# Weight loads for the second expert, weight splits and number conversions at other steps, and a branch hint for two more engines

## The chip, the cores and the metric

The kernel runs on one core of a Trainium2 chip as one launch. The metric is the device time of a run in microseconds (us), the median over several runs. The core's engines have queues of their own, and the text calls them as the profile does: PE (matrix engine), PEld (its weight loads), DVE (vector), ACT (scalar), POOL (GpSimd) and SP (which here issues the weight loads). A trailing q, as in PEq, means the engine's sequencer: branches, semaphore waits and the like.

## The reference, cut to what matters

```
attn_out = _attn_ref(q, k, v, omega)          # 4 x 8 heads x 576 x 64, random features
x = attn_out ... reshape(2304, 512)
x = (x @ w_a * (x @ w_b)) @ w_out             # MoE 1: 512 -> 1536 -> 512, dense
logits = normalised x @ normalised expert_emb.T / tau
expert_idx = argmax(logits, axis=1)           # 8 experts
out[mask] = gate_w[mask] * (relu(x[mask] @ w1[e]) @ w2[e])   # MoE 2: w1 512x1024, w2 1024x512
```

All inputs are float32. Each product is made of three TensorE products, with every operand split into a rounded high part and the remainder.

## The kernel before

**Attention** (to about 198 us) and the conversion of the MoE 1 weights run first. The weights of w_a, w_b and w_out come in as 36 pieces (3 for each of 12 chunks `kf`) through a small staging ring `stg` and are rebuilt on the chip, one piece by one call of `conv()`: an ACT pass (line 235), two DVE passes `cv<-stg` (lines 236 and 238) and a POOL addition (line 240). When the 36th is done, `load_en` fetches the normalised expert embeddings back.

**MoE 1** runs over 6 units `u` of 384 tokens and, within each, the 12 chunks `kf`; step n is 12u + kf, and the first `ND` = 5 steps lie in the attention. In the loop of `run` each step n issues, in this order: the conversions that are due (the `while` of line 1153, whose formula decides how many each step gets), the split of the next chunk's weights (`chunk_ab`: ACT cast `abh`, line 562, and DVE subtraction `abl`, line 563), 24 matmuls `pA`, `pB` of this chunk (`ab_mm`, lines 595 to 597), the product `h` on DVE (line 611), its split `hh`, `hl`, and 9 matmuls `pO` (`out_mm`, line 627), of this or an earlier step. Each engine executes its instructions in the order in which the loop issues them. In units 1 to 5 DVE, ACT and POOL also compute the routing of the unit before (`route_plan`: scores in kf 1 to 8, softmax in kf 9, ranks and scatters behind).

In the last unit, kf 0 calls `alloc_stage` and loads both weights of the most used expert e0 into the staging tiles `st` (`load_w`: 4 DMAs of 512 KB for w1, line 901, and 8 of 256 KB for w2, line 905). At kf 8, 9, 10 and 11 a quarter of w1 each is split into `w1t` pairs (ACT cast and DVE subtraction of 128x1024).

**MoE 2** has a step 0 (320 tokens of e0), a step 1 (256 tokens of e0), and then bodies `body_b(j)`, of up to 16, one for each block of up to 320 tokens of one expert. In this input 7 run (`nB` = 7), and three experts occur. A step takes hidden blocks `p_h` (w1) and output blocks `p_o` (w2, tiles `w2t` and `w2u`), gathers rows by indirect DMAs on POOL (`rid`, then `xr<-yd,rid`), and scatters its result (`out_dram<-ob`). `after` is a piece of code that a step calls late: in step 0 it loads w1 of the second expert e1, in step 1 it is `first`, which loads w2 of that expert (and w1 only if the guess of e1 was wrong, `hn > 0`), and in the bodies it loads both weights of the expert after. The staging tiles are freed by the splits of the expert before. Bodies from `NSB_MIN` = 5 on stand in nested `If(nB > j)`, line 1313. Which width of a body runs is a branch on `kind` (lines 1298 and 1299). PE has a prefetch hint for the branch of line 1299 (`hint(j)`); no other engine has hints.

Of the kernel before, what the change touches and what calls it, by code (L numbers as in the profile page):

```python
# [17 lines left out]
ENG = mybir.EngineType  # L18
# [8 lines left out]
NU = NTILE // TU  # L27
KF = DFF // 128
# [4 lines left out]
NSB = 16  # L33
NSB_MIN = 5
NPRE = 24
# [4 lines left out]
ND = 5  # L40
# [60 lines left out]
class Kern:  # L101
# [790 lines left out]

    def alloc_stage(s):
        t = [s.x6("st", F32, (128, 1536)) for _ in range(6)]
        s.st1 = [t[k // 1][:, 0:1024] for k in range(4)]
        s.st2 = [t[k][:, 1024:1536] for k in range(4)] + [t[4][:, k:k + 512] for k in (0, 512, 1024)] + [t[5][:, 0:512]]
        s.x2 = t[5][:, 512:512 + XW]
# [12 lines left out]

    def alloc_w1(s):
        W = lambda: s.ab([128, 1024], F32R, "w1t")
        s.w1s = [(W(), W()) for _ in range(4)]

    def alloc_w2(s):
        W = lambda: s.ab([128, 2, 512], F32R, "w2t")
# [205 lines left out]
    def run(s):  # L1122
        nc, tc = s.nc, s.tc
        s.setup_consts()
        s.p0_consts()
        s.conv_open()
        x, ch, wo, hr, hs = {}, {}, {}, {}, {}

        def prep(n):
            if n in hr:  # L1130
                hs[n] = s.split_h(hr.pop(n))

        for t in s.attention():
            if TS - 2 <= t < TS:
                if t == TS - 2:
                    x[0], th = s.split_x(s.xraw[0])
                th.pop(0)()
            k, r = divmod(t - TS, TD)
            if 0 <= k < ND and r == 0:
                hr[k] = s.ab_mm(s.chunk_early(k), x[0])  # L1140
        xraw = s.xraw
        steps = [(u, kf) for u in range(NU) for kf in range(KF)]
        R = {}
        todo = {}
        en = s.setup_en()
        ch[ND] = s.chunk_ab(ND)
        done = 0
        for n, (u, kf) in enumerate(steps):
            if n < ND:
                continue  # L1150
            if n == ND:
                yield
            while s.n_conv < 3 * KF and s.n_conv < max(3 * (n + 2), NPRE + (3 * KF - NPRE) * (n + 1 - ND) // (KF - 2 - ND)):
                s.conv()
                if s.n_conv == 3 * KF:
                    s.load_en()
            next(en, None)
            if n + 1 < len(steps):
                ch[n + 1] = s.chunk_ab(steps[n + 1][1])
            if kf in (10, 11) and u + 1 < NU:  # L1160
                if kf == 10:
                    x[u + 1], xth = s.split_x(xraw[u + 1])
                xth.pop(0)()
            for f in todo.get(kf, []):
                f()
            if n == ND:
                wo[0] = s.chunk_wo(0)
                prep(0)
            hr[n] = s.ab_mm(ch.pop(n), x[u])
            if n - done <= 1:  # L1170
                prep(n)
            for f in todo.get(kf + 0.5, []):
                f()
            goal = n if u else (KF - 1) * (n + 1 - ND) // (KF - ND)
            while done < goal:
                s.out_mm(wo.pop(done), hs.pop(done), steps[done][1])
                done += 1
                wo[done] = s.chunk_wo(steps[done][1])
                prep(done)
            if kf == 0:  # L1180
                todo = s.route_plan(u - 1, R) if u else {}
            if u == NU - 1 and kf == 0:
                s.alloc_stage()
                s.load_w(s.e0v)
            if u == NU - 1 and kf == 8:
                s.alloc_w1()
            if u == NU - 1 and kf in (8, 9, 10, 11):
                s.split(*s.w1s[kf - 8], s.st1[kf - 8])
            if u == NU - 1 and kf == 6:
                s.alloc_x()  # L1190
                for i in range(SA):
                    s.ids_of(i, [s.idxa[:, t:t + 1] for t in range(3 * i, 5 if i else 3)])
            if u == NU - 1 and kf == 7:
                for i in range(SA):
                    for t in range(2 if i else 3):
                        s.gather(i, t, NT - 2 * TU * 128)
        n = len(steps) - 1
        s.alloc_p2()
        s.p_h = [s.psum("A", "p_h") for _ in range(3)]
        for t in range(3):  # L1200
            s.xT(0, t, s.p_h[t])
        s.out_mm(wo.pop(n), hs.pop(n), KF - 1)
        s.alloc_w2()
        s.split2(0, 4)
        s.alloc_h()
        s.queue_route(NU - 1, R)
        L = lambda ap, eng, hi: nc.values_load(ap, engines=eng, min_val=0, max_val=hi)  # L1207
        AD = [ENG.Activation, ENG.DVE]
        s.slot_now, s.early = 0, False
        ids_b = lambda j: s.ids_of(SA + j, [s.idxb[:, j, t:t + 1] for t in range(3)])  # L1210

        def idx_ready():
            if s.slot_now < 1:
                s.early = True
                return
            ids_b(0)
            for t in range(3):
                s.gather(SA, t)

        s.idx_ready = idx_ready  # L1220

        def next_xT(i, j):

            k = L(s.kind[0:1, j:j + 1], [ENG.PE] + AD, 2)

            def third(p, rest):
                with s.tc.If(k > 1) as c:
                    s.xT(i, 2, p[2])
                    rest()
                with c.Else():  # L1230
                    rest()
            return lambda p: xT2(i, p), third

        def xT2(i, p):
            for t in range(2):
                s.xT(i, t, p[t])

        s.step(0, 2, split2=lambda a, b: s.split2(a, b) if a else None, after=lambda: s.load_w1(s.e1v), nextx=lambda: (lambda p: xT2(1, p), None), bg=BG[0])
        s.slot_now = 1
        if s.early:  # L1240
            idx_ready()

        def hint(j):

            if j < NSB:
                k = L(s.kind[0:1, j:j + 1], [ENG.PE], 2)
                tc.mark_branch_hint_location(f"wide{j}", hint=k // 2, engines=[ENG.PE])

        def first():
            s.pump(1000)  # L1250
            s.alloc_b()
            ids_b(1)
            with tc.block():
                hint(0)
            hn = L(s.n0i[0:1, 1:2], [ENG.SP], 1)
            ne = L(s.n0i[0:1, 0:1], [ENG.SP], E - 1)
            with tc.If(hn > 0):
                s.load_w1(ne)
            s.load_w2(ne)

        def first1(f):
            f0 = L(s.fl[0:1, 0, 0:1], AD, 1)
            with tc.If(f0 > 0):
                s.split1(f)

        s.step(1, 1, after=first, split1=first1, nextx=lambda: next_xT(SA, 0), bg=BG[1])
        nB = L(s.nB[0:1, 0:1], mybir.ALL_ENGINES, NSB)

        def body_b(j):
            i = SA + j  # L1270
            new = L(s.fl[0:1, 0, j:j + 1], AD, 1)
            last = L(s.fl[0:1, 0, j + 1:j + 2], AD, 1)
            kind = L(s.kind[0:1, j:j + 1], mybir.ALL_ENGINES, 2)
            hn = L(s.fl[0:1, 1, j:j + 1], [ENG.SP], 1)
            ne = L(s.fl[0:1, 2, j:j + 1], [ENG.SP], E - 1)
            nx = None
            if j + 1 < NSB:
                for t in range(3):
                    s.gather(i + 1, t)
                x = next_xT(i + 1, j + 1)  # L1280
                nx = lambda: x
            if j + 2 < NSB:
                ids_b(j + 2)

            def sp2(a, b):
                with tc.If(new > 0):
                    s.split2(a, b)

            def sp1(f):
                with tc.If(last > 0):  # L1290
                    s.split1(f)

            def after():
                with tc.If(hn > 0):
                    s.load_w(ne)
                hint(j + 1)

            with tc.If(kind > 0) as c:
                with tc.If(kind > 1, label=f"wide{j}") as d:  # L1299
                    s.step(i, 2, sp2, sp1, after, nx)  # L1300
                with d.Else():
                    s.step(i, 1, sp2, sp1, after, nx)
            with c.Else():
                s.step(i, 0, sp2, sp1, after, nx)

        def rec_b(j):
            if j == NSB:
                return
            if j < NSB_MIN:
                body_b(j)  # L1310
                rec_b(j + 1)
            else:
                with tc.If(nB > j):  # L1313
                    body_b(j)
                    rec_b(j + 1)

        rec_b(0)
# [90 lines left out]
```

## Time and profile before

| | |
|---|---|
| median of 3 runs | 902.41 us (898.89, 902.41, 902.68) |
| the profiled execution's own time | 901.02 us |
| its span in the trace | 899.1 us |
| mean granted TensorE clock | 0.981 of full speed |
| busy: PE, DVE, ACT, POOL | 838.5, 595.2, 452.7, 348.6 us |

The span reaches from the first to the last traced instruction; the own time holds 1.9 us more. PE is busy 93% of the span, so time can go only where PE waits, where its clock is low, or after its last instruction.

### The profile page before, as it was taken

The page shows a single profiled execution, that of the slowest core. Times are in us where ns is not written, and L with a number is a line of the kernel's source. Part 1 is how long each engine was busy: PE and PEld are TensorE (multiplying, and loading weights), DVE is VectorE, ACT ScalarE, POOL GpSimd, SP SyncE. Part 2 cuts the span into 40 slices and gives each one's busy share as a digit, 9 for nine tenths or more (in the row PEclk, how much of TensorE's full clock was granted, in tenths as well). Part 3 has the DMA queues.
Part 4 walks back from the last instruction along what each step waited for, and adds up shares of the span by engine and source line. Part 5 has one row for each costly group of instructions (what it writes and reads, how often), then busy time and mean ns, then how long its engine had stood idle before and what let it go on. Part 6 is the DMA issues. An engine that isn't in the chain of part 4 may idle for free. (4 is left out here: it accounts for less than half of the span.)

```text
span 899.1 us, 15947 instructions
## 1 busy us (share of the span) xinstructions
PE 838.5 (93%) x5783; PEld 760.7 (85%) x5783; DVE 595.2 (66%) x1294; ACT 452.7 (50%) x1039; POOL 348.6 (39%) x332
## 2 busy tenths in 40 slices
PE   6989898899899999999999999999999799899991
PEld 5878787798799999999999999999888688799971
DVE  5899999857957865876786686687756434422220
ACT  4779888676445546545554654554622323311110
POOL 6576876503404313402512531255213433333330
PEclk9999999999999999999999999999999899999996
DMA  9564854302300010000001000502133721122220
GB/s 222 179 195 132 239 160 130 99 8 92 114 30 1 1 37 1 1 37 1 1 1 37 0 1 37 188 2 61 37 118 117 238 95 51 58 63 62 63 64 16
DMA packets 68355, 67.14 MB, mean 75 GB/s; under 512 B 27552, under 2 KB 56608, under 8 KB 68096
## 3 DMA queue, kind: packets, MB, share of 16 engines
q1 hardware_dynamic: 62784, 52.90, 19.4%
q0 software_dynamic: 5440, 12.68, 4.7%
q8 instruction: 60, 0.98, 0.5%
q14 instruction: 71, 0.58, 0.2%
HBM read 55.88 MB, written 9.68 MB: 73 GB/s over the span
## 5 line engine op out<-in xcount | busy, mean ns | idle before, releaser
L660 POOL TENSOR_TENSOR trp<-y,en 128x512 f32<-128x512 f32 x60 | 90.3, 1520 | 122.5 <-ACT trp L661 68.5
L1035 PE MATMUL p_h<-xth,w1t 128*128 128x256 f32 (+1 forms) x512 | 101.2, 293 | 7.9 <-DVE w2t L563 4.6
L562 ACT CAST hh<-h 128x384 fp32r<-128x384 f32 x72 | 37.1, 515 | 127.7 <-DVE h L611 127.7
L563 DVE TENSOR_TENSOR abl<-ab,abh 128x1024 fp32r<-128x1024 f32 x67 | 87.1, 1300 | 20.9 <-ACT abh L562 20.3
L597 PE MATMUL pB<-xuh,abl 128*128 128x384 f32 x288 | 96.9, 336 | 0.0
L390 ACT ACTIVATE p<-pj,nb 128x128 f32<-128x128 f32 x288 | 80.2, 396 | 26.2 <-DVE nb L379 16.1
L597 PE MATMUL pA<-xuh,abl 128*128 128x384 f32 x268 | 90.0, 336 | 1.4 <-DVE abl L563 1.4
L1035 PEld LDWEIGHTS p_h<-xth,w1t 128*128 128x128 f32 x512 | 83.1, 193 | 9.4 <-issue 9.1
L596 PE MATMUL pA<-xul,abh 128*128 128x384 f32 x268 | 90.1, 336 | 0.0
L595 PE MATMUL pA<-xuh,abh 128*128 128x384 f32 x268 | 90.1, 336 | 0.0
L595 PE MATMUL pB<-xuh,abh 128*128 128x384 f32 x268 | 89.5, 334 | 0.0
L596 PE MATMUL pB<-xul,abh 128*128 128x384 f32 x268 | 89.5, 334 | 0.0
L611 DVE TENSOR_TENSOR h<-pB,a 128x384 f32<-128x384 f32 x72 | 39.7, 552 | 63.3 <-PE pB L597 35.9
L1015 ACT ACTIVATE hT<-p_h 128x512 fp32r<-128x512 f32 (+1 forms) x42 | 22.5, 539 | 105.8 <-PE p_h L1035 70.9
L1035 PE MATMUL p_h<-xtl,w1t 128*128 128x256 f32 (+1 forms) x256 | 74.9, 293 | 0.0
L1020 DVE SCALAR_TENSOR_TENSOR hT<-p_h,hT 128x256 fp32r<-128x256 f32 (+2 forms) x52 | 25.0, 504 | 72.4 <-ACT hT L1015 42.5
L562 ACT CAST abh<-ab 128x1024 fp32r<-128x1024 f32 x67 | 70.3, 1049 | 0.5 <-PE pB L596 0.5
L653 DVE CUSTOM_DVE_ANT_0 trv<-y,en 128x512 bf16<-128x512 f32 x60 | 66.4, 1107 | 0.7
L627 PE MATMUL pO<-woh,hl 128*128 128x512 f32 x216 | 63.2, 401 | 2.8 <-DVE hl L563 2.8
L563 DVE TENSOR_TENSOR hl<-h,hh 128x384 fp32r<-128x384 f32 x72 | 40.5, 562 | 34.9 <-ACT hh L562 34.9
L627 PE MATMUL pO<-woh,hh 128*128 128x512 f32 x216 | 62.8, 399 | 0.4 <-ACT woh L562 0.4
L627 PE MATMUL pO<-wol,hh 128*128 128x512 f32 x216 | 62.5, 398 | 0.0
(237 smaller groups left out, 2133.9 us busy)
## 6 DMA issues: line engine op xcount, KB each, us to landing
stg<-in_moe_w_a_dram SPq DMA_DIRECT2D x12, 512.0 KB
stg<-in_moe_w_b_dram SPq DMA_DIRECT2D x12, 512.0 KB
stg<-in_moe_w_out_dram SPq DMA_DIRECT2D x12, 512.0 KB
st<-in_moe_w_dram SPq DMA_DIRECT2D x12, 512.0 KB
st<-in_moe_w_dram SPq DMA_DIRECT2D x24, 256.0 KB
yd<-y SPq DMA_DIRECT2D x6, 792.0 KB
v<-in_v_dram SPq DMA_DIRECT2D x16, 256.0 KB
q<-in_q_dram SPq DMA_DIRECT2D x8, 512.0 KB
```

The costliest lines, as they stand in the source:

```text
L390: s.nc.scalar.activation(out=s.p_[j][:, 4 * half + n], in_=pj[:, n * M:n * M + M], func=ACTF.Exp, bias=nb[:, n:n + 1])
L562: s.nc.scalar.copy(out=hi, in_=src)
L563: s.nc.vector.tensor_tensor(out=lo, in0=src, in1=hi.bitcast(F32), op=ALU.subtract)
L595: mm(out=out, lhsT=ah, rhs=wh, start=st, stop=False)
L596: mm(out=out, lhsT=ah, rhs=wl, start=False, stop=False)
L597: mm(out=out, lhsT=al, rhs=wh, start=False, stop=sp)
L611: nc.vector.tensor_tensor(out=h, in0=pp[1][:, :N], in1=a, op=ALU.mult)
L627: s.nc.tensor.matmul(out=s.po[j], lhsT=a[:, j * 128:j * 128 + 128], rhs=b, start=st, stop=sp)
L653: nc.vector.tensor_tensor_reduce(out=tr, in0=y[:, j, :DM], in1=s.en[:, e], scale=1.0, scalar=0.0, op0=ALU.mult, op1=ALU.add, accum_out=dt[ ...
L660: nc.gpsimd.tensor_tensor(out=tr, in0=y[:, j, :DM], in1=s.en[:, e], op=ALU.mult)
L1020: nc.vector.scalar_tensor_tensor(out=v, in0=pv[:, a - k0:b - k0], scalar=0.0, in1=h, op0=ALU.max, op1=ALU.subtract)
L1035: return lambda: nc.tensor.matmul(out=out, lhsT=a, rhs=b, start=st, stop=sp, skip_group_check=True)
```

## The change

It consists of four edits. In the MoE 1 loop the conversions are spread over one more step: the divisor in the formula becomes `KF - 1 - ND`. The four splits of w1 of e0 move from kf 8, 9, 10, 11 to kf 5, 7, 9, 11, and behind the last of them the loop now issues the four DMAs for w1 of e1. Step 0's `after` loads w2 of e1 in the place of w1, and `first` loads both only if the guess was wrong. Bodies from 4 on begin with a small block that gives POOL and DVE a prefetch hint on whether the next nested `If` is taken.

```
--- before.py
+++ after.py
@@ -892,6 +892,7 @@
 
     def alloc_stage(s):
         t = [s.x6("st", F32, (128, 1536)) for _ in range(6)]
+        s.w1s = []
         s.st1 = [t[k // 1][:, 0:1024] for k in range(4)]
         s.st2 = [t[k][:, 1024:1536] for k in range(4)] + [t[4][:, k:k + 512] for k in (0, 512, 1024)] + [t[5][:, 0:512]]
         s.x2 = t[5][:, 512:512 + XW]
@@ -910,7 +911,7 @@
 
     def alloc_w1(s):
         W = lambda: s.ab([128, 1024], F32R, "w1t")
-        s.w1s = [(W(), W()) for _ in range(4)]
+        s.w1s.append((W(), W()))
 
     def alloc_w2(s):
         W = lambda: s.ab([128, 2, 512], F32R, "w2t")
@@ -1150,7 +1151,7 @@
                 continue
             if n == ND:
                 yield
-            while s.n_conv < 3 * KF and s.n_conv < max(3 * (n + 2), NPRE + (3 * KF - NPRE) * (n + 1 - ND) // (KF - 2 - ND)):
+            while s.n_conv < 3 * KF and s.n_conv < max(3 * (n + 2), NPRE + (3 * KF - NPRE) * (n + 1 - ND) // (KF - 1 - ND)):
                 s.conv()
                 if s.n_conv == 3 * KF:
                     s.load_en()
@@ -1182,10 +1183,12 @@
             if u == NU - 1 and kf == 0:
                 s.alloc_stage()
                 s.load_w(s.e0v)
-            if u == NU - 1 and kf == 8:
+            if u == NU - 1 and kf in (5, 7, 9, 11):
+                k = (kf - 5) // 2
                 s.alloc_w1()
-            if u == NU - 1 and kf in (8, 9, 10, 11):
-                s.split(*s.w1s[kf - 8], s.st1[kf - 8])
+                s.split(*s.w1s[k], s.st1[k])
+                if k == 3:
+                    s.load_w1(s.e1v)
             if u == NU - 1 and kf == 6:
                 s.alloc_x()
                 for i in range(SA):
@@ -1235,7 +1238,7 @@
             for t in range(2):
                 s.xT(i, t, p[t])
 
-        s.step(0, 2, split2=lambda a, b: s.split2(a, b) if a else None, after=lambda: s.load_w1(s.e1v), nextx=lambda: (lambda p: xT2(1, p), None), bg=BG[0])
+        s.step(0, 2, split2=lambda a, b: s.split2(a, b) if a else None, after=lambda: s.load_w2(s.e1v), nextx=lambda: (lambda p: xT2(1, p), None), bg=BG[0])
         s.slot_now = 1
         if s.early:
             idx_ready()
@@ -1255,8 +1258,7 @@
             hn = L(s.n0i[0:1, 1:2], [ENG.SP], 1)
             ne = L(s.n0i[0:1, 0:1], [ENG.SP], E - 1)
             with tc.If(hn > 0):
-                s.load_w1(ne)
-            s.load_w2(ne)
+                s.load_w(ne)
 
         def first1(f):
             f0 = L(s.fl[0:1, 0, 0:1], AD, 1)
@@ -1268,6 +1270,9 @@
 
         def body_b(j):
             i = SA + j
+            if NSB_MIN <= j + 1 < NSB:
+                with tc.block():
+                    tc.mark_branch_hint_location(f"more{j + 1}", hint=nB > j + 1, engines=[ENG.Pool, ENG.DVE])
             new = L(s.fl[0:1, 0, j:j + 1], AD, 1)
             last = L(s.fl[0:1, 0, j + 1:j + 2], AD, 1)
             kind = L(s.kind[0:1, j:j + 1], mybir.ALL_ENGINES, 2)
@@ -1310,7 +1315,7 @@
                 body_b(j)
                 rec_b(j + 1)
             else:
-                with tc.If(nB > j):
+                with tc.If(nB > j, label=f"more{j}"):
                     body_b(j)
                     rec_b(j + 1)
```

The first place is DVE in unit 0 of MoE 1, near step 7. `cv<-stg` rows are conversions, `abl` the split of the next chunk, `h` the product.

```order
 L236 TENSOR_SCALAR cv<-stg 128x512
 L238 SCALAR_TENSOR_TENSOR cv<-stg,cv 128x512
-L236 TENSOR_SCALAR cv<-stg 128x512
-L238 SCALAR_TENSOR_TENSOR cv<-stg,cv 128x512
 L563 TENSOR_TENSOR abl<-ab,abh 128x1024
 L611 TENSOR_TENSOR h<-pB,a 128x384
```

One of three conversions left this step. One more leaves step 9 in the same way, and both come back in step 10:

```order
 L563 TENSOR_TENSOR hl<-h,hh 128x384
+L236 TENSOR_SCALAR cv<-stg 128x512
+L238 SCALAR_TENSOR_TENSOR cv<-stg,cv 128x512
+L236 TENSOR_SCALAR cv<-stg 128x512
+L238 SCALAR_TENSOR_TENSOR cv<-stg,cv 128x512
 L563 TENSOR_TENSOR abl<-ab,abh 128x1024
 L563 TENSOR_TENSOR xul<-xraw,xuh 128x768
```

Step 10 had no conversion before; now two stand ahead of its `abl`. The steps 5, 6 and 8 keep their two each.

The second place is SP, between the end of MoE 1 and step 0 of MoE 2. `yd<-y` are the last results of MoE 1 going to memory, a 128x1024 `st` is a quarter of w1, a 128x512 `st` an eighth of w2 (the changed file's line numbers are one higher here).

```order
 L701 DMA yd<-y 128x3x528
+L902 ISA
+L902 DMA st<-in_moe_w_dram 128x1024
+L902 ISA
+L902 DMA st<-in_moe_w_dram 128x1024
+L902 ISA
+L902 DMA st<-in_moe_w_dram 128x1024
+L902 ISA
+L902 DMA st<-in_moe_w_dram 128x1024
 L98 DMA yd<-y 128x3x528
```

The w1 load of e1 moved ahead of the last `yd<-y`; behind that row, where it stood, the eight DMAs of w2 stand now.

The third place is POOL at the start of body 4, behind the last scatter of body 3 in the program's text. It had this:

```order
L1117 DMA out_dram<-ob,xr 2304x512
L1298 ISA
L1298 UNCONDITIONAL_BRANCH
L1207 TENSOR_LOAD tb
L981 DMA xr<-yd,rid 128x528 x2
```

It now has this:

```order
L1118 DMA out_dram<-ob,xr 2304x512
L1303 ISA
L1303 UNCONDITIONAL_BRANCH
L1275 REGISTER_ALU
L1409 BRANCH_PREFETCH_HINT
L1274 UNCONDITIONAL_BRANCH
L1210 TENSOR_LOAD tb
L982 DMA xr<-yd,rid 128x528 x2
```

A comparison, the hint and a branch out of the block were added. DVE has the same three; PE, ACT and SP have only the added unconditional branch.

## Rows read from the trace of the kernel before

**Rows 1.** PE timeline, 223 to 237 us: start, duration, operation, idle before and releaser.
```profile
224.85 0.44 PE L597 MATMUL pA<-xuh,abl 128*128 128x384 f32 x1 [0.26 <-DVE abl L563]
...
234.51 1.65 PE L627 MATMUL pO<-woh,hl 128*128 128x512 f32 x3 [2.77 <-DVE hl L563]
```

**Rows 2.** DVE timeline, 217 to 225 us.
```profile
218.89 0.69 DVE L238 SCALAR_TENSOR_TENSOR cv<-stg,cv 128x512 int32<-128x512 int32 x1
...
221.55 0.41 DVE L236 TENSOR_SCALAR cv<-stg 128x512 int32<-128x512 int32 x1
222.00 1.67 DVE L238 SCALAR_TENSOR_TENSOR cv<-stg,cv 128x512 int32<-128x512 int32 x1
```

**Rows 3.** Windows: length, busy PE, PEld, DVE, ACT, POOL; PEclk; DMA; GB/s.
```profile
234.20:237.60 3.40, 3.09 (x8) 2.07 (x9) 1.60 (x4) 0.54 (x1) 0.00 (x0) 0.50 0.00 0
708.60:715.50 6.90, 5.22 (x24) 5.25 (x25) 2.32 (x4) 0.00 (x0) 2.04 (x2) 0.51 0.64 211
...
771.60:776.00 4.40, 4.38 (x37) 4.40 (x38) 2.73 (x5) 0.60 (x1) 3.48 (x4) 1.00 0.49 138
```

**Rows 4.** Timeline of all engines, 248 to 252 us.
```profile
248.66 0.56 DVE L611 TENSOR_TENSOR h<-pB,a 128x384 f32<-128x384 f32 x1 [0.70 <-PE pB L597]
...
249.73 0.55 DVE L563 TENSOR_TENSOR hl<-h,hh 128x384 fp32r<-128x384 f32 x1
...
251.20 0.86 PE L627 MATMUL pO<-woh,hl 128*128 128x512 f32 x3
```

**Rows 5.** PE timeline, 622 to 640 us, the rows with a wait.
```profile
626.86 0.44 PE L597 MATMUL pA<-xuh,abl 128*128 128x384 f32 x1 [0.50 <-DVE abl L563]
...
631.42 0.97 PE L627 MATMUL pO<-woh,hh 128*128 128x512 f32 x3 [0.39 <-ACT woh L562]
...
634.77 0.44 PE L597 MATMUL pA<-xuh,abl 128*128 128x384 f32 x1 [0.63 <-DVE abl L563]
```

**Rows 6.** DVE timeline, 604 to 638 us.
```profile
609.14 3.62 DVE L563 TENSOR_TENSOR abl<-ab,abh 128x1024 fp32r<-128x1024 f32 x1 [0.26 <-ACT abh L562]
...
625.59 1.22 DVE L563 TENSOR_TENSOR abl<-ab,abh 128x1024 fp32r<-128x1024 f32 x1
```

**Rows 7.** PE timeline, first matmul of body 0 and of body 2.
```profile
710.28 0.55 PE L1035 MATMUL p_h<-xth,w1t 128*128 128x256 f32 x1 [4.60 <-DVE w2t L563]
...
771.62 0.36 PE L1035 MATMUL p_h<-xth,w1t 128*128 128x256 f32 x1 [3.29 <-issue]
```

**Rows 8.** Line 1299 near 703, 764 and 839: count, duration ns min/median/max, first, last.
```profile
L1299 PEldq COMPARE_BRANCH  x1: 6890/6890/6890, 703.2 to 703.2; - x1
...
L1299 PEldq COMPARE_BRANCH  x2: 2127/3020/3914, 764.0 to 769.3; - x2
...
L1299 PEldq COMPARE_BRANCH  x1: 351/351/351, 839.6 to 839.6; - x1
```

**Rows 9.** SP timeline around steps 0 and 1: the loads for e1 (w2) and e2 (w1).
```profile
689.65 5.02 SPq L905 DMA_DIRECT2D st<-in_moe_w_dram  x8
...
699.10 2.68 SPq L901 DMA_DIRECT2D st<-in_moe_w_dram  x4
```

**Rows 10.** DMA view, 700 to 709 us: packets, MB, share of the 16 engines.
```profile
q1 hardware_dynamic: 572, 2.09, 66.5%
q0 software_dynamic: 270, 0.55, 16.4%
```

**Rows 11.** Windows as in Rows 3, at the end of step 1.
```profile
706.00:708.00 2.00, 0.00 (x0) 0.00 (x0) 0.47 (x1) 0.99 (x2) 0.00 (x0) 1.00 0.83 318
708.00:710.00 2.00, 0.00 (x0) 0.00 (x0) 1.58 (x3) 0.00 (x0) 0.00 (x0) 0.66 0.11 37
```

**Rows 12.** Lines 1313 and 1404 from 870 us on; columns as in Rows 8.
```profile
L1313 POOLq EVENT_SEMAPHORE  x5: 17/43/43, 887.2 to 887.6; - x5
...
L1313 POOLq COMPARE_BRANCH  x2: 43/46/50, 884.3 to 889.9; - x2
...
L1404 POOLq DRAIN  x3: 50/107/8239, 890.0 to 898.8; - x3
```

More of the change, by code (lines that the diff above doesn't have):

```diff
@@ L894, in alloc_stage @@
         t = [s.x6("st", F32, (128, 1536)) for _ in range(6)]
+        s.w1s = []
         s.st1 = [t[k // 1][:, 0:1024] for k in range(4)]
@@ L912, in alloc_w1 @@
         W = lambda: s.ab([128, 1024], F32R, "w1t")
-        s.w1s = [(W(), W()) for _ in range(4)]
+        s.w1s.append((W(), W()))
     def alloc_w2(s):
@@ L1152, in run @@
                 yield
-            while s.n_conv < 3 * KF and s.n_conv < max(3 * (n + 2), NPRE + (3 * KF - NPRE) * (n + 1 - ND) // (KF - 2 - ND)):
+            while s.n_conv < 3 * KF and s.n_conv < max(3 * (n + 2), NPRE + (3 * KF - NPRE) * (n + 1 - ND) // (KF - 1 - ND)):
                 s.conv()
@@ L1184, in run @@
                 s.load_w(s.e0v)
-            if u == NU - 1 and kf == 8:
+            if u == NU - 1 and kf in (5, 7, 9, 11):
+                k = (kf - 5) // 2
                 s.alloc_w1()
-            if u == NU - 1 and kf in (8, 9, 10, 11):
-                s.split(*s.w1s[kf - 8], s.st1[kf - 8])
+                s.split(*s.w1s[k], s.st1[k])
+                if k == 3:
+                    s.load_w1(s.e1v)
             if u == NU - 1 and kf == 6:
@@ L1236, in xT2 @@
                 s.xT(i, t, p[t])
-        s.step(0, 2, split2=lambda a, b: s.split2(a, b) if a else None, after=lambda: s.load_w1(s.e1v), nextx=lambda: (lambda p: xT2(1, p), None), bg=BG[0])
+        s.step(0, 2, split2=lambda a, b: s.split2(a, b) if a else None, after=lambda: s.load_w2(s.e1v), nextx=lambda: (lambda p: xT2(1, p), None), bg=BG[0])
         s.slot_now = 1
@@ L1257, in first @@
             with tc.If(hn > 0):
-                s.load_w1(ne)
-            s.load_w2(ne)
+                s.load_w(ne)
         def first1(f):
@@ L1270, in body_b @@
             i = SA + j
+            if NSB_MIN <= j + 1 < NSB:
+                with tc.block():
+                    tc.mark_branch_hint_location(f"more{j + 1}", hint=nB > j + 1, engines=[ENG.Pool, ENG.DVE])
             new = L(s.fl[0:1, 0, j:j + 1], AD, 1)
@@ L1312, in rec_b @@
             else:
-                with tc.If(nB > j):
+                with tc.If(nB > j, label=f"more{j}"):
                     body_b(j)
```

## The prediction

> **What bounds the kernel now.** The page's engine list comes first: PE is busy 93% of the span, no other engine over 66% but PE's own weight loads. So time can be had where PE waits, where its clock is low, or behind its last instruction. The chain of waits that ends last runs over the row gathers of the experts and does not show where PE loses time, so I read PE's timeline for rows with a wait ahead, then the windows for the clock, then the queue rows at the waits. The change touches four places.
>
> (A) In unit 0 of MoE 1 PE waits 0.26 us at 224.85 for `abl` and 2.77 at 234.51 for `hl`, both from DVE [rows 1]. Behind the second wait the granted clock is 0.50 for 3.40 us, the 1.2 GHz level, with 3.09 us of PE work in it [rows 3]; that work would have taken half as long at 2.4 GHz, so the fall costs 1.55.
>
> (B) In the last unit PE waits 0.50, 0.39 and 0.63 us [rows 5], 1.52 together.
>
> (C) Before body 0 PE waits 4.60 us, to 710.28 [rows 7]. The view puts this down to DVE's `w2t`, but the row that tells it is the branch of line 1299: PE's sequencer sat 6.89 us in it from 703.2, where the same line takes 2.1 to 3.9 at 764 to 769 and 0.35 at 839.6 [rows 8]. DMA was 0.83 busy in 706 to 708 and 0.11 in the two us behind [rows 11]; PE went on when the traffic was over. I take the branch to wait for its code, which comes by DMA, behind weights. The clock is then 0.51 for 6.90 us with 5.22 us of PE work [rows 3]: 2.6 lost. Together this place costs 7.2.
>
> (D) Behind PE's end POOL reaches its branch of line 1313 at 884.3 and its next semaphore instruction at 887.2, 2.9 us with nothing in between; it drains for 8.24 us from 890.0, and the span ends behind that [rows 12].
>
> **A: conversions.** Step 7 loses one of three conversions. Its DVE passes take 0.41 + 1.67 = 2.08 us (0.41 + 0.69 = 1.10 where the second pass is quick) [rows 2]. DVE runs through without a pause here, so everything behind comes 2.08 earlier, and so does the end of the wait at 234.51, which shrinks to 2.77 + 0.26 - 2.08 = 0.95. The waits of 0.39 to 0.63 [rows 5] are the nearest in size to it, and I take no fall of the clock behind it: 2.08 + 1.55 = 3.63. The price is step 10, which had no conversion and gets two, 2.2 to 4.2 us of DVE by the same passes, ahead of the `hl` that ended at 250.28 and was wanted at 251.20 [rows 4]: 0.92 of cover, and DVE has 0.70 of idle time shortly before [rows 4]. That makes 0.6 to 2.5 late; the quick pass is the rule where POOL is idle, as it mostly is there, so I take 0.6. A = 3.63 - 0.6 = **3.0**; bounds -0.4 (2.08 gained, 2.5 lost, and the clock falls once more in the new place) and 3.6. What else moves with it, ACT's and POOL's shares of the conversions and the fetch of the embeddings by one step, lies on engines half idle.
>
> **B: splits of w1.** A split is an ACT cast ahead of `abh` and a DVE pass of the size of `abl`, 1.22, ahead of `abl` [rows 6]. The waits of 0.50 and 0.39 lie behind the split of kf 8 and go with it; that of 0.63 lies behind kf 9, which keeps its split, so I leave 0.55 of it. Kf 5 and 7 now take one each. PE shows no wait in those steps, so they have slack, but DVE's `abl` took 3.62 at 609.14 instead of 1.22, near POOL's gathers [rows 6]. A slow pass there would eat the gain. B = **1.0**; bounds -1.5 (one pass 2.4 too long, 0.9 of it covered) and 1.5.
>
> **C: weight loads.** The w2 load of e1 went out on SP from 689.65 to 694.67, 2 MB, and the w1 load of e2 from 699.10 [rows 9]. The second is freed by the splits of step 1 and does not move. The first moves to the place of the w1 load of e1 behind step 0, and that one to the end of MoE 1. The early loads themselves remove no wait, since none is seen on e1's weights; I cost them at nothing, hidden by the matmuls of MoE 1's end and of steps 0 and 1, which work on resident weights (without that cover a load of 2 MB is 5.5 us, by the rate below). What remains is second-hand: with 689.65 to 697 free, the three row gathers come earlier. They are 0.55 MB of the 2.64 MB that moved in 700 to 709 [rows 10]. At 318 GB/s for a share of 0.83, thus 383 GB/s [rows 11], 0.55 MB are 1.45 us. The 2.09 MB of w1 alone take 5.5 us, to 704.6 if they start at 699.10, against an end near 706 + 0.83 x 2 = 707.7 now: 3.1. Between 1.45 and 3.1 I take 2.0: PE resumes near 708.3 instead of 710.28. Work behind the branch, body 0's first 24 rows of `p_h`, waits that much less. The stall is then still about 3. Behind 2.77 the clock fell for 3.40 us (a loss of 1.55); behind 3.29 at 771.62 it stayed at 1.00 [rows 3, 7]. I count 1.55 as left of 2.6: 1.05 saved. C = **3.05**; bounds 0 and 7.2.
>
> The Trainium skill (DMA: Bandwidth & Descriptors, section Queues, rings and completion order) says that a DMA engine takes turns between its queues packet by packet; by that a code block would not wait for a whole weight load, and C would be 0. The row of 6.89 us that ends with the traffic speaks against it, so it stays a rival.
>
> **D: hints.** A hinted PE branch took 2.1 or 2.0 three times and 0.35 or 0.32 twice, against 3.9 without [rows 8]: 1.85 or 3.55 less. Of POOL's gap of 2.9 [rows 12] that makes 1.85 three times and 2.6 twice, mean 2.15. The trace has no hinted POOL branch. D = **2.1**; bounds 0 (the drain ends by something else) and 2.6. The hint's own three instructions per body lie on POOL and DVE, which wait for PE there; uncovered, three of some 46 ns [rows 12] in three bodies would be 0.4 us.
>
> **Sum.** 3.0 + 1.0 + 3.05 + 2.1 = 9.15 from the profiled execution's own 901.02: 891.9. The median shown lies 1.4 above that execution, and one run 2.1 below it; I add 0.6: **892.5**.
>
> **Rivals.** (1) The branch before body 0 keeps its 6.9 us, because the load that it waits behind (w1 of e2) stays where it is, or because a block of code never waited for a whole load, the engines taking turns between queues. For it: that load is issued at 699.10 as before. Against: a fifth of the bytes that move with it goes. C = 0: 895.5.
> (2) With the early traffic gone the code block comes before the weights, and the stall and the fall of the clock both vanish, as at 839.6 with its 0.35. C = 7.2: 888.3. Against: the fetch would have to be ahead of 699.1, and PE enters the branch at 703.2.
> (3) The hints do nothing for the end, because POOL's drain waits for a fixed event, or the prefetched code is displaced by the many branches between. D = 0: 894.6. For it: of the 8.24 us drain no row shows what it waits for.
> (4) Slower: the block around the hint adds an unconditional branch on PE at the start of bodies 4, 5 and 6. If each fetches code like the 3.91 us branch [rows 8], that is up to 11.7 on PE, and 891.9 + 11.7 = 903.6, with the same 0.6 904.2. It decides from 9.2 on, thus three full misses. Against: the target is the next instruction, and PE has queued matmuls to work off.
> (5) The change does not do what it says: w2 of e1 was early enough before, and A gives back in step 10 what it gains in step 7. Then B and D alone, 898.5.
>
> The Trainium skill (Runtime: NRT & Kernel Launch, section Instruction fetch mechanics) says that a branch out of the two code pages at hand costs a DMA fetch of 16 KB. By that the added branch to the next instruction costs nothing, and (4) falls; no run here shows it yet.
>
> **How the numbers follow.** All steps as summed 0.42; (1) 0.19; (2) 0.10; (3) 0.13; (4) 0.05; (5) 0.11. The likeliest is the sum, 892.5. The range is to leave out no more than 2 in 10: below it reaches past (2)'s 888.3 to 887.0, for the open bounds of A; above it takes in (1), (3) and most of (5), to 898.5. About 0.5%, 4.5 us, can be told from no change, so faster is below 897.9 and slower above 906.9. Faster: the sum, (1) to (3), 0.84, less 0.07 for their tails, 0.77; within 0.5%: (5), most of (4) and the tails, 0.19; slower: a tail of (4), with A's lower bound, 0.04.
>
> **What would show it.** A: at about 232 to 235 PE waits under 1.2 us, and the clock is full in all of unit 0; a wait for `hl` or `abl` near step 10 is under 1 us. B: one wait above 0.3 is left in kf 8 to 10, none in kf 5 to 8. C: the branch of line 1299 into body 0 is near 5 us, DMA goes quiet near 706, and PE waits near 3. D: POOL's first semaphore instruction behind its last branch follows in under 1 us, and the end of the span comes 2 us sooner after the last scatter. The forecast is wrong if the 6.89 stays though DMA is quiet before it ends (then the branch waits for something else), if the clock falls in a new place, or if PE's branches in bodies 4 to 6 grow.

## The result, and the profile after

The changed kernel takes 893.03 us (median of 6 runs, 892.3 to 894.11) against 902.54 before (6 runs beside them, 898.89 to 903.06): ratio 0.9903, 95% interval 0.9885 to 0.992, thus 9.5 us less. Measured twice more, on two chips and each time beside the kernel before, it stood at 0.9964 (0.9947 to 0.998) and 0.9949 (0.9929 to 0.9969), 3 to 5 us less. The sign is the same each time, but the size differs by several us, and the experiments show where that comes from.

PE's timeline of the changed kernel, the rows with a wait (start, duration, operation, idle before and releaser), answers to [rows 1, 5, 7]:

```profile
231.79 0.97 PE L627 MATMUL pO<-woh,hl 128*128 128x512 f32 x3 [1.27 <-DVE hl L563]
248.62 0.96 PE L627 MATMUL pO<-woh,hl 128*128 128x512 f32 x3 [1.38 <-DVE hl L563]
...
609.72 0.96 PE L627 MATMUL pO<-woh,hl 128*128 128x512 f32 x3 [0.17 <-DVE hl L563]
631.05 0.44 PE L597 MATMUL pA<-xuh,abl 128*128 128x384 f32 x1 [0.34 <-DVE abl L563]
...
704.71 0.55 PE L1036 MATMUL p_h<-xth,w1t 128*128 128x256 f32 x1 [2.92 <-issue]
765.04 0.36 PE L1036 MATMUL p_h<-xth,w1t 128*128 128x256 f32 x1 [3.16 <-issue]
...
862.34 0.70 PE L1036 MATMUL p_h<-w1t,xth 128*128 128x512 f32 x2 [1.80 <-DVE ob L1116]
```

The wait of 2.77 became 1.27, and one of 1.38 is new, in step 10. Two of the three waits in the last unit went, the third is 0.34, and a small one of 0.17 is new. Before body 0 PE waits 2.92 instead of 4.60. The windows of the same trace (columns as in [rows 3]):

```profile
231.80:235.00 3.20, 3.20 (x17) 2.63 (x18) 2.11 (x5) 1.14 (x2) 0.00 (x0) 1.00 0.00 0
248.60:252.00 3.40, 3.38 (x17) 3.11 (x18) 3.04 (x4) 1.13 (x2) 0.00 (x0) 1.00 0.40 169
703.00:709.00 6.00, 4.29 (x24) 4.32 (x25) 2.50 (x4) 0.41 (x1) 2.25 (x2) 0.72 0.36 109
765.00:769.50 4.50, 4.46 (x25) 4.49 (x26) 2.50 (x4) 0.00 (x0) 3.58 (x4) 0.62 0.59 142
```

The clock is full behind both waits of unit 0. It falls for a shorter time in body 0 (mean 0.72 over 6 us), and in a place where it had not fallen before, behind the wait at 765. The branch into body 0 (it was line 1299, [rows 8]) and POOL's end ([rows 12]), with duration in ns and first and last start:

```profile
L1304 PEldq COMPARE_BRANCH  x1: 5188/5188/5188, 699.4 to 699.4; - x1
```

```profile
L1318 POOLq EVENT_SEMAPHORE  x5: 17/43/43, 879.2 to 879.5; - x5
L1318 POOLq COMPARE_BRANCH  x3: 39/43/70, 863.6 to 881.9; - x3
...
L1409 POOLq DRAIN  x3: 46/113/8233, 882.1 to 890.9; - x3
```

POOL's branch behind the last scatter stands at 878.6 in the trace and its next semaphore instruction at 879.2: 0.6 instead of 2.9 us. The drain is as long as it was.

Since the same matmul can be found in both traces, the difference of its starts tells how much was won up to it. Each step below is the change of that difference:

| up to | before | after | difference | won in this stretch |
|---|---|---|---|---|
| matmul 2200, ahead of all edits | 216.87 | 216.18 | -0.69 | 0.7, not from the change |
| behind the first wait of unit 0 (A, step 7) | 240.03 | 235.92 | -4.11 | 3.4 |
| second wait of unit 0 (A, step 10) | 251.20 | 248.62 | -2.58 | -1.5 |
| wait behind kf 9 (B) | 634.77 | 631.05 | -3.72 | 1.1 |
| first matmul of body 0 | 710.28 | 704.71 | -5.57 | 1.9 |
| first matmul of body 2 (C) | 771.62 | 765.04 | -6.58 | 1.0 |
| first matmul of body 6 | 867.15 | 862.34 | -4.81 | -1.8 |
| end of the span (D) | 899.1 | 891.1 | -8.0 | 3.2 |

Of the loss of 1.8, 1.5 lie right behind the wait at 765, where the clock fell anew: the same two matmuls stand at 771.62 and 776.09 before, at 765.04 and 771.02 after. So 8.0 is the sum of A 1.9 (3.4 won, 1.5 given back), B 1.1, C 2.9, D 3.2, 0.7 of the start of the program and -1.8.

The waits of A and B stand in all further traces of the changed kernel too: 1.25 to 1.27 and 1.38 to 1.39 in unit 0, 0.16 to 0.18 and 0.33 in the last unit.

### The profile page after: what moved, and what is told of

The parts are those of the page before. It is cut to its first block, busy times and chain, and to the rows that moved or that the text cites. A ratio compares the mean times of both kernels' runs of the same rounds, so it can differ in the third digit from the quotient of the medians.

```text
span 891.1 us, 15971 instructions
## 1 busy us (share of the span) xinstructions
PE 837.4 (94%) x5783; PEld 760.1 (85%) x5783; DVE 595.5 (67%) x1294; ACT 451.9 (51%) x1039; POOL 349.8 (39%) x332
## 5 line engine op out<-in xcount | busy, mean ns | idle before, releaser
L390 ACT ACTIVATE p<-pj,nb 128x128 f32<-128x128 f32 x288 | 80.0, 398 | 25.8 <-DVE nb L379 15.5
L563 DVE TENSOR_TENSOR hl<-h,hh 128x384 fp32r<-128x384 f32 x72 | 43.3, 602 | 34.8 <-ACT hh L562 34.2
```

The costliest lines, as they stand in the source:

```text
L390: s.nc.scalar.activation(out=s.p_[j][:, 4 * half + n], in_=pj[:, n * M:n * M + M], func=ACTF.Exp, bias=nb[:, n:n + 1])
L563: s.nc.vector.tensor_tensor(out=lo, in0=src, in1=hi.bitcast(F32), op=ALU.subtract)
```

## The experiments

**Each edit alone.** Four kernels, each the one before with one of the four edits, all on one chip.

The conversions alone:

```
- (n + 1 - ND) // (KF - 2 - ND)
+ (n + 1 - ND) // (KF - 1 - ND)
```

> The kernel before with the new spread of the conversions alone. By matched matmuls of the two traces the spread gains about 3.1 us near step 7 and gives 1.4 back near step 10. Theory: -1.7 us on the time (0.9981), with waits of about 1.3 us near 232 and 1.4 near 249 and no fall of the clock behind either. Rival, the sum as predicted: -3.0 us, with a wait of 0.6 in step 10. Rival, nothing: the give-back near step 10 grows to 3 us with a fall of the clock.

Measured 0.9989 (0.9963 to 1.0015): too small to tell from nothing by the time. PE's timeline of this kernel shows the mechanism:

```profile
231.78 0.95 PE L627 MATMUL pO<-woh,hl 128*128 128x512 f32 x3 [1.25 <-DVE hl L563]
248.60 0.96 PE L627 MATMUL pO<-woh,hl 128*128 128x512 f32 x3 [1.38 <-DVE hl L563]
```

The same two waits as in the changed kernel, and the second row starts 2.60 earlier than the one at 251.20 did, of which 0.68 was there ahead of the edit (matmul 2200 at 216.19): 1.9 us, near the theory of 1.7 and not the predicted 3.0.

The four splits at kf 5, 7, 9 and 11 alone, loads where they were:

```
- if u == NU - 1 and kf in (8, 9, 10, 11):
-     s.split(*s.w1s[kf - 8], s.st1[kf - 8])
+ if u == NU - 1 and kf in (5, 7, 9, 11):
+     k = (kf - 5) // 2
+     s.alloc_w1()
+     s.split(*s.w1s[k], s.st1[k])
  ...      # alloc_w1 now makes one pair a call
```

> The kernel before with the four w1 splits at kf 5, 7, 9 and 11 alone, loads where they were. Theory: the waits of 0.50 and 0.39 behind kf 8 go, that behind kf 9 shrinks to about 0.35, -1.1 us (0.9988). Rival: the pieces now in kf 5 and 7 meet slow DVE passes near POOL's gathers, a new wait of about 0.4 us appears near 610 and the gain is 0.7 or less.

Measured 0.9979 (0.9958 to 1.0). Its PE timeline in the last unit has two waits left:

```profile
611.61 0.97 PE L627 MATMUL pO<-woh,hl 128*128 128x512 f32 x3 [0.21 <-DVE hl L563]
632.93 0.45 PE L597 MATMUL pA<-xuh,abl 128*128 128x384 f32 x1 [0.31 <-DVE abl L563]
```

Both expectations saw a part: the new wait near 610 is there but small, and the rest goes. By matched matmuls 1.1 us is won up to the second, so the theory holds in the trace; the time alone can't tell it from nothing.

The loads alone (w1 of e1 behind the split of kf 11, w2 behind step 0):

```
  s.split(*s.w1s[kf - 8], s.st1[kf - 8])
+ if kf == 11:
+     s.load_w1(s.e1v)
- after=lambda: s.load_w1(s.e1v)
+ after=lambda: s.load_w2(s.e1v)
  with tc.If(hn > 0):
-     s.load_w1(ne)
- s.load_w2(ne)
+     s.load_w(ne)
```

> The kernel before with the earlier loads of the second expert alone (w1 behind the split of kf 11, w2 behind step 0). Theory, the branch into body 0 waits for code behind weight traffic and the traffic ends earlier: its branch takes about 5.2 us instead of 6.9, PE's wait there about 3.0 instead of 4.6, the half-clock stretch is 3.4 us instead of 6.9, together -2.7 us (0.997). Rival, the gain at this place in the changed kernel comes from other edits (code moved by the hints, PE's time against the loads): branch 6.9 and wait 4.6 as before, 0 us.

Measured 1.001 (0.9982 to 1.0038): no gain is seen, and the theory's 0.997 lies outside the interval. The branch into body 0 took 6.11 us, from 704.9, between the two expectations, and in PE's timeline stands a wait in step 1 that neither theory knew:

```profile
698.89 1.66 PE L1035 MATMUL p_o<-w2u,hT 128*128 128x512 f32 x6 [2.08 <-issue]
711.22 0.35 PE L1035 MATMUL p_h<-xth,w1t 128*128 128x256 f32 x1 [3.93 <-DVE w2t L563]
```

In this trace PE goes on behind its branch at 711.2 though DMA has not gone quiet: the window ahead (columns as in [rows 3]) shows it 0.95 busy.

```profile
709.00:711.00 2.00, 0.00 (x0) 0.00 (x0) 0.77 (x2) 0.61 (x2) 0.00 (x0) 1.00 0.95 371
```

The hints alone:

```
+ if NSB_MIN <= j + 1 < NSB:
+     with tc.block():
+         tc.mark_branch_hint_location(f"more{j + 1}", hint=nB > j + 1, engines=[ENG.Pool, ENG.DVE])
  ...      # and the label of the If that it names
```

> The kernel before with the hints for GpSimd and VectorE alone. Theory: GpSimd's gap behind its branch near 884 falls from 2.9 to about 0.55 us, -2.3 us (0.9975), its drain stays at 8.2. Rival: the gain is 3.0, as VectorE's last result also starts 0.7 sooner behind the last matmul. Rival: the drain ends by something else, 0 us.

Measured 0.9984 (0.9961 to 1.0008). From PE's last matmul (its end at 880.9) to the end of the span 16.3 us pass; it was 18.0 in the three kernels without hints and 18.9 in the trace before. All fourteen traces say the same: from POOL's branch to its next semaphore instruction it is 0.55 us in the ten with hints and 2.69 to 2.93 in the four without, the drain behind it is 8.23 to 8.24 in all, and the tail behind PE is 15.5 to 16.9 against 18.0 to 18.9. The hints are worth 1.7 to 2.3; what the trace of before had beyond that, some 0.9, was its own. This trace also shows that A's second part was not certain: here the same wait of 2.77 us as in [rows 1] is followed by a full clock, while it fell in the kernels with the splits or the loads alone.

```profile
234.00:238.00 4.00, 3.93 (x21) 3.37 (x22) 2.83 (x7) 0.28 (x1) 0.51 (x1) 1.00 0.00 0
```

The four ratios add up to -0.4%, 3.4 us (-0.11, -0.21, +0.1 and -0.16%), near the smaller of the three results of the whole change; but each is uncertain by some 0.2 to 0.3%, about 2 us, so the traces carry the argument here and not this sum.

**The branch into body 0.** The next four ran on a second chip. The first is the changed kernel again. The second makes the weights that the branch meets come later, by their order on SP:

```
  with tc.If(hn > 0):
-     s.load_w(ne)
+     s.load_w2(ne, range(4))
+     s.load_w1(ne)
+     s.load_w2(ne, range(4, 8))
  ...      # load_w2 takes the pieces to load
```

> The changed kernel once more, as the measure for the next three on the same chip. Expected 0.990 of the time before, two waits of about 1.3 us in unit 0, a branch of 5.2 us into body 0. Where the short stretches at half clock fall is expected to differ from the first trace.

> The changed kernel, but in the bodies half of the next expert's w2 is asked for ahead of its w1, so that SP waits for body 0's splits before any of that traffic starts and the branch into body 0 meets quiet queues. Theory, the code comes late because it shares the DMA engines with the weights: the branch falls from 5.2 us to 2.0 (hint works) or 3.9 (it does not), PE's wait from 2.9 to 0.3 or less, or to 1.6; -1.3 to -4.4 us against the changed kernel. Rival, the branch has another cause: it stays at 5.2. Rival, the load comes too late for the splits of that expert: a new wait of several us near 765.

Measured 0.9964 (0.9947 to 0.998) for the changed kernel, not the 0.990 expected, and 0.9921 (0.9896 to 0.9946) with the late load. The branch in the one and in the other:

```profile
L1304 PEldq COMPARE_BRANCH  x1: 6848/6848/6848, 702.5 to 702.5; - x1
```

```profile
L1306 PEldq COMPARE_BRANCH  x1: 3868/3868/3868, 701.6 to 701.6; - x1
```

Without weight traffic the branch takes 3.87 us, as the one of 3.91 in [rows 8], and PE's wait fell from 4.34 to 1.35. So the code does come late because of the weights; the theory holds, with its second number (no help from PE's hint here). But in the changed kernel the branch was 6.85 this time, and not 5.19. PE's wait near 765 is no longer than it was (3.05): the load was not too late for its splits.

The code itself can be seen in the traces: the DMA view counts instruction packets, and those on queue q8 are of 16 KB each and go with PE's branches (columns as in [rows 10]). In the kernel before, while PE stands in the branch from 703.2, the window 703.2 to 707.7 has none; the next, 707.7 to 708.8, has one:

```profile
q1 hardware_dynamic: 401, 1.45, 82.2%
q0 software_dynamic: 144, 0.19, 11.6%
q14 instruction: 1, 0.01, 0.4%
```

```profile
q0 software_dynamic: 33, 0.07, 17.3%
q1 hardware_dynamic: 9, 0.02, 7.2%
q8 instruction: 1, 0.02, 5.6%
```

It starts at 707.75 and lands at 708.73, and the branch ends at 710.12. In all fourteen traces the branch into body 0 ends 1.2 to 1.5 us behind the landing of this packet, and the packet itself takes 1.0 to 1.4. What differs is its start: 1.9 to 4.6 us behind PE's arrival at the branch in the ten traces with e2's w1 load under way, 0.6 to 1.6 in the four with that load moved behind. So the branch waits for its code, and the code for its turn. It need not wait for the end of the load: its packet starts 0.6 to 3.0 us before the load's last packet lands.

Both traces have a wait in step 1 as the one with the loads alone: 2.53 and 2.62 us. What stands behind it is on ACT, whose `hT` waits for the last `p_h` group of step 1. In the changed kernel's first trace and in this one:

```profile
688.88 0.60 ACT L1016 ACTIVATE hT<-p_h 128x512 fp32r<-128x512 f32 x1 [2.19 <-PE p_h L1036]
```

```profile
694.92 0.60 ACT L1016 ACTIVATE hT<-p_h 128x512 fp32r<-128x512 f32 x1 [8.21 <-remote]
```

PE's last `p_h` matmul of that group is over at 688.87 in this second trace, and PE's next products run on behind it until they want `hT`. The event that should have let ACT go reached it 6.0 us later. "remote" means that the trace knows no instruction that ended the wait at that time. In the kernel before the group is over at 692.53 and this `hT` starts 1.7 behind it:

```profile
694.26 0.60 ACT L1015 ACTIVATE hT<-p_h 128x512 fp32r<-128x512 f32 x1 [3.88 <-PE p_o L1035]
```

This event also sets when e2's w1 load begins: in the ten traces without the late load it begins 4.8 to 5.0 us behind the start of this `hT` (688.88 and 693.73 in the changed kernel's first trace, 694.26 and 699.10 before, 698.24 and 703.06 with the loads alone).

A third kernel of this set takes one conversion out of step 10 and puts it into step 9 (2, 2, 2, 2, 3, 1 over steps 5 to 10):

```
- NPRE + (3 * KF - NPRE) * (n + 1 - ND) // (KF - 1 - ND)
+ NPRE + (2, 4, 6, 8, 11, 12)[min(n - ND, 5)]
```

> The changed kernel with the conversions spread 2, 2, 2, 2, 3, 1 over steps 5 to 10 in place of 2 each. Theory, the two conversions in step 10 make its hl late: with one the wait of 1.38 us near 249 goes, and step 9 takes three without a wait as before; -1.4 us against the changed kernel. Rival: one conversion of 2.1 us still exceeds the cover, a wait of about 0.4 stays, -1.0. Rival: the wait moves to step 9, 0.

> Both of these edits together. Theory: the sum of the two, -2.7 to -5.8 us against the changed kernel, thus 0.984 to 0.987 of the time before.

Measured 0.9958 (0.9939 to 0.9976) and, with the late load too, 0.9925 (0.99 to 0.9949), neither told apart from the kernel without this edit. The wait near 249 did not go:

```profile
247.42 0.97 PE L627 MATMUL pO<-woh,hl 128*128 128x512 f32 x3 [0.99 <-DVE hl L563]
```

1.38 became 0.99: halving the conversions there takes only 0.4 off. The trace shows why. DVE has hardly a pause from the passes of step 9 to this `hl`, 15.26 us busy of 15.40, so a conversion moved from step 10 to step 9 still stands ahead of it:

```profile
232.00:247.40 15.40, 14.43 (x76) 12.59 (x74) 15.26 (x21) 7.40 (x13) 7.88 (x6) 1.00 0.26 99
```

The changed kernel has one pause in the same stretch, 0.57 us for ACT's `abh`, and a slow `abl` behind it, 1.98 instead of 1.22:

```profile
244.19 1.98 DVE L563 TENSOR_TENSOR abl<-ab,abh 128x1024 fp32r<-128x1024 f32 x1 [0.57 <-ACT abh L562]
```

The kernel with both edits was no faster than with the late load alone, against an expected 0.984 to 0.987. Its profiled execution was the slowest of its six (897.44, median 894.44); in it the event in step 1 came 8.9 us late and PE waited 5.3 there.

**Is the late event made by the moved loads?** Up to here it was late by 1.3 to 2.3 us in the four traces without the moved loads, by 4.2 to 8.9 in five with them, and by nothing in one, the changed kernel's first. The last four ran on a third chip: the changed kernel, the same with e1's w2 back in `first`, that with the late load, and the late load as above.

```
- s.step(0, ..., after=lambda: s.load_w2(s.e1v), ...)
+ s.step(0, ..., after=lambda: None, ...)
  with tc.If(hn > 0):
-     s.load_w(ne)
+     s.load_w1(ne)
+ s.load_w2(ne)
```

> The changed kernel a third time, as the measure for the next three. In its second trace the event that ends the last p_h group of step 1 came 6.0 us after that group's matmuls and PE then waited 2.5 us near 695; in its first trace it came at once. Expected: late by 4 us or more again, ratio to the kernel before 0.990 to 0.997.

> The changed kernel with the w2 load of the second expert back in first of step 1, its w1 load left early. Theory: the late event in step 1 comes with the moved w2 load (4 to 9 us in five of six traces with it, 1 to 2.5 in four of four without), so here it is late by 1 to 2.5 us and PE does not wait near 695; the branch into body 0 is 6 to 7 us again; the time is that of the changed kernel within 1 us, or up to 2.5 below. Rival: the lateness has nothing to do with that load; it stays at 4 us or more, and the time rises by the longer branch.

> As the run before, and with the w1 load of the third expert behind half of its w2. Theory, both waits are gone: no wait near 695, a branch of 3.9 us into body 0 and a wait of about 1.3 there; 4 to 6 us below the changed kernel, 2 below the one with the late w1 load alone. Rival: the event is late all the same and the time is that of the late w1 load alone.

> The changed kernel with the late w1 load of the third expert once more. Expected: a branch of 3.9 us into body 0, a wait near 694 of 2 to 5 us behind the late event, 3 to 4 us below the changed kernel.

| | ratio to before (interval) | event late | branch into body 0 | PE's wait there |
|---|---|---|---|---|
| changed kernel | 0.9949 (0.9929 to 0.9969) | 0.04 | 6.42 | 4.09 |
| w2 back | 0.9939 (0.9915 to 0.9963) | 0.04 | 4.37 | 1.95 |
| w2 back, late load | 0.9919 (0.9894 to 0.9945) | 0.04 | 4.03 | 1.75 |
| late load | 0.9893 (0.9869 to 0.9917) | 0.04 | 2.93 | 0.60 |

The event was on time in all four, with the moved w2 load and with it back, so these expectations missed. My theory that the moved w2 load makes it late falls as a cause: the changed kernel has it at 0.04 here. Whether it is late at all differs between the sets, for a reason that no run shows; whether the moved loads lengthen it where it is late stays open, and there is no trace of the kernel before on this chip.

The first two lines of the table tell more of the branch. The w1 load of e2 began at the same time in both, 693.86 and 693.90; PE came to the branch at 698.5 in the one and, behind a wait for gathered rows, at 700.6 in the other; and it left it at the same time, 704.9 (698.5 + 6.42, 700.6 + 4.37). In SP's timeline and in the branch row of the kernel with w2 back:

```profile
685.91 4.27 SPq L906 DMA_DIRECT2D st<-in_moe_w_dram  x8
693.90 2.36 SPq L902 DMA_DIRECT2D st<-in_moe_w_dram  x4
```

```profile
L1305 PEldq COMPARE_BRANCH  x1: 4371/4371/4371, 700.6 to 700.6; - x1
```

So in these two the end of the branch goes with the begin of this load, not with what moved ahead of it or when PE came: here e1's w2 went out from 685.91 to 690.18, right ahead, and the branch ended no later for it (the code packet started at 702.41 and 702.49). It is no fixed distance: over the ten traces under that load the branch ends 8.0 to 11.1 us behind its begin. The gathers did come later (that wait for rows was 1.55 us), but PE would only have stood in the branch instead.

The late load shows most in the last line, whose profiled execution was the fastest of its six (886.31). PE's first row in body 0, the windows around the branch, and SP's loads in that kernel:

```profile
701.57 0.35 PE L1036 MATMUL p_h<-xth,w1t 128*128 128x256 f32 x1 [0.60 <-ACT w2t L562]
```

```profile
697.00:699.00 2.00, 2.00 (x11) 1.60 (x10) 1.42 (x4) 0.59 (x3) 1.39 (x3) 1.00 0.02 4
699.00:701.00 2.00, 1.97 (x9) 1.27 (x7) 0.00 (x0) 0.48 (x1) 0.74 (x1) 1.00 0.38 138
...
701.50:708.00 6.50, 6.43 (x54) 6.46 (x55) 3.36 (x6) 2.21 (x5) 3.79 (x4) 1.00 0.53 174
```

```profile
704.29 2.30 SPq L906 DMA_DIRECT2D st<-in_moe_w_dram  x4
706.78 3.38 SPq L902 DMA_DIRECT2D st<-in_moe_w_dram  x4
```

No weight traffic runs while the branch waits, the loads start 3 us after it, and the clock stays full in body 0. This kernel is the fastest of all: 888.62 us against 894.18 for the changed one and 898.3 for the one before, on the same chip, 5.6 below the changed one where 3 to 4 were expected. With the w2 load back as well it was 2.8 below, where 4 to 6 were expected.

## Why the prediction was right, point by point

The forecast was 892.5, the time 893.03. The sum came out, but not each of its terms.

**A, 3.0, measured 1.9.** The mechanism was right on both sides: the wait near 234 shrank and the clock did not fall behind it, and step 10 got a wait for `hl`. The gain at step 7 was 3.4 where 3.63 was worked out (the wait ended 2.03 earlier, the forecast said 2.08). What was mis-sized is the price in step 10: 1.5 where 0.6 was taken, within the 0.6 to 2.5 given. I took the quick pass for both conversions; one of the two second passes took 1.67, DVE paused 0.57 for ACT's `abh`, and `abl` took 1.98. That the clock would fall behind 2.77 us was not certain either, as the trace with the hints alone shows.

**B, 1.0, measured 1.1.** As worked out, except that kf 9's wait shrank to 0.34 by itself and kf 7 took 0.2. The slow pass beside POOL's gathers ate little.

**C, 3.05, 2.9 in the first trace: right in the number, and that step failed.** I reasoned that with e1's loads gone from the stretch ahead, the w1 load of e2 would end 2.0 us earlier and the code with it. That the code comes late under weight traffic is shown: with that load moved away the branch takes 2.9 to 4.0 us in four traces, under it 4.4 to 7.0 in ten, and the code packet's late start is the difference. PE does not wait for the traffic to be over, as I read it: with the loads alone it left the branch at 711.05 and the load's last packet landed at 711.67. But the load does not end earlier: from its begin to its last packet it is 8.8 to 10.7 us in four traces without the moved loads (mean 9.7) and 8.6 to 11.7 in five with them (mean 9.8).

Nor do the moved loads shorten the branch. It took 5.19, 6.85, 6.42 and 6.99 us in the traces with all of the change (6.11 with the loads alone) and 6.89, 6.04, 6.61 and 6.36 without. The two short ones, 5.19 and 4.37 (the latter with w2 back), are those where PE came latest behind the begin of e2's load, 5.6 and 6.7 us; both ended about 11 us behind it, as before the change (699.10 to 710.1), so they were short because PE came late and not because the code came early. From the wait behind kf 9 to the first matmul of body 2, by rows as those shown, 136.9, 134.3, 136.2 and 136.7 us pass without the moved loads (mean 136.0) and 134.0, 138.9, 135.3, 138.4 and 136.7 with them (mean 136.6). Three of these five hold the wait behind the late event; the other two, 134.0 and 135.3, and the 132.7 of the kernel with w2 back, leave room for a gain of 0.7 to 3.3 us where the event is on time, but no trace of the kernel before has it on time to compare. Rival (1), that this load stays where it is and C is nothing, described the kernel better. The 2.9 of the first pair is then a matter of these two executions: e2's load began 5.4 us earlier in the second (699.10, 693.73) and PE came to the branch only 3.9 earlier (703.2, 699.4), and the clock fell for 6.8 us in the one and 3.4 in the other. The event that frees the splits ahead of that load was late by 1.7 in the first and on time in the second. In both the load begins 4.8 us behind the `hT` that this event lets go, so the event set the load's earlier begin; why it came on time stays open.

The page of the Trainium skill that I set against this step (DMA: Bandwidth & Descriptors, section Queues, rings and completion order) says that an engine takes turns between queues by packets. The trace with the loads alone agrees in so far as the code came while DMA was still 0.95 busy; but its packet started 3.7 us behind PE's arrival there, against 0.6 to 1.6 with that load moved away, so taking turns did not spare it the wait.

**D, 2.1, measured 3.2 in the first pair.** The gap behind POOL's branch fell from 2.9 to 0.6, 2.3 us; by PE's last matmul 1.7 to 2.3 are the hints'. The rest was in the trace of before alone. The drain stayed and the end still came sooner, so rival (3) falls. Rival (4), new fetches on PE by the added branch, falls too: the DMA view counts 60 instruction packets on q8 in both kernels, and between body 2 and body 6 little was lost beyond the clock's 1.5.

**What the forecast left out** is that last loss: a fall of the clock behind the wait of 3.16 before body 2, which I had named only as a sign of error. And the kernel before varies by itself, 898.9 to 903.1 in one set of six runs. So of the 9.5 measured, about 5 are shown to be the change's own (A 1.9, B 1.1, D 2.0), and the other two sets, 3 to 5 us, agree. That the first one met the forecast of 892.5 so closely was luck: C's 2.9, 0.9 of D and 0.7 of the start, none of them shown to be the change's, made up for what A and the clock's new fall took away.

## What to carry to other kernels

In this kernel a branch that needed new code paid for what the DMA queues held when it came. Look at which bulk load is in flight at such a branch and when the instruction packet starts, and move that load, not those ahead of it; here an order on SP gave about as much again as the four edits together (0.9893 against 0.9949, and 0.9921 against 0.9964). And a gain at a wait is worth what its trace says plus or minus the clock's fall behind it, so a term that rests on one trace's fall should carry a chance and not its whole price.

## What the runs showed that I had not expected

The event that ends a group of matmuls in step 1 reached ACT 0.04 us behind the matmuls in five of the fourteen traces (the changed kernel's first and all four of the last set) and 1.3 to 8.9 us behind them in the other nine, at the same group each time. PE did not wait at that place up to 2.3 us late, and 0.7 to 5.3 beyond; but in the seven of the nine without the late load e2's w1 load began later with it. What holds it up stays open.

The granted clock does not follow from the length of a wait alone. Behind 2.77 to 2.79 us near 234 it fell to 1.2 GHz in three traces of four; behind about 3 us before body 2 it fell in the changed kernel's first trace (3.16) and neither in its second (3.11) nor before the change (3.29). From there to PE's end a fall lasted 3.4 or 6.8 us.
